# Wider products, a filter split by channels, filter sums on TensorE and whole x * v units per engine, in a fused long convolution and gated MLP

## The chip, the cores and the metric

One core of one Trainium2 chip. The metric is the device time of one execution in microseconds (us). Engines are named as the profile names them: PE is TensorE's matmuls, PEld its weight loads, DVE is VectorE, ACT ScalarE, POOL GpSimd, SP the engine that issues the DMAs. A ratio is the mean time of one kernel's fast runs over that of the other's fast runs of the same rounds, so it is not quite the ratio of the medians beside it. A difference of under 2% counts as "same".

## The reference, cut to what matters

```python
u = x * v                                    # 4 batches x 12480 positions x 128 channels, fp32
h = relu(pos_emb @ w1) @ w2 * exp(-0.01*pos) # the filter, one for all batches
y = irfft(rfft(u, 2*S) * rfft(h, 2*S))[:S]   # a long convolution for each channel
z = (x * y).reshape(49920, 128)
g = z @ w_in;  out = (g * cos(g)) @ w_out    # d_ff = 2048: "the MoE"
```

The kernel does the convolution as a two-level transform. In its **first step** (`f1`) it multiplies by a cosine and sine table. In the **second step** (`f2`) it multiplies by a table `w` that differs for each row `k`, and takes the complex product with the filter's spectrum `h`. The **third step** (`i1`) and the **last** (`i2`) go back. The filter's and batch 0's second steps run together (the **joint** second step) and leave `w` and `h` in DRAM. Batches 1 to 3 load them again and run interleaved with the MoE of the batches before (the **later** second steps).

## The kernel before: the parts that the change and the argument touch

```python
def u_load(pool, bufs, b, a):                # bufs is 3: three x buffers, two v buffers
    for name, src, n in (("xt", x, bufs), ("vt", v, bufs - 1)):
        ...                                  # one DMA each
def u_sums(u, tiles, a):                     # sum on GpSimd, difference on VectorE
    for place, op, e in ((a, ALU.add, nc.gpsimd), (ODD + a, ALU.subtract, nc.vector)):
        e.tensor_tensor(...)
first_u = u_units(0, 3, slots[0:R, :, :, :], # who multiplies which half of x * v
                  lambda j, half: nc.vector if half and j % 3 and j < 18 else nc.gpsimd)

def f2_mm(ps, w, k1, i, filt=False):         # 2 rows k per unit
    ...
    elif k < KF:                             # filter: one product of 256 columns
        nc.tensor.matmul(pi, w[:, i, :], both, start=True, stop=True)
    else:                                    # or two of 128
        for r, src in enumerate((ftile[0:KE, :, k, :], above[0:KE, :, k - KF, :])):
            nc.tensor.matmul(pi[:, r * D:(r + 1) * D], w[:, i, :], src, ...)

def f2_product(pool, ps, h, k1):             # each yield ends a step of the interleaving
    t = pool.tile([N2, 2, CB, 2, 2], F32, name="t", bufs=1)
    for r, op in ((0, ALU.subtract), (1, ALU.add)):
        nc.vector.tensor_tensor(y[:, r], uu[:, 0], hh[:, r], op=ALU.mult)
        yield
        nc.vector.tensor_tensor(t[:, r], uu[:, 1], hh[:, 1 - r], op=ALU.mult)
        nc.gpsimd.tensor_tensor(y[:, r], y[:, r], t[:, r], op=op)
        yield
# joint step: w has 2 buffers and is stored to DRAM, h has 3 and is stored too
```

In the later second steps the code between two yields is a piece of the interleaving: a unit has four, and they are spread over 2.9 steps of the MoE (`F2_STEPS` in the kernel), so most steps of the MoE have one piece beside them and some two. The MoE's chain crosses all engines: PE `ph`, ACT `a`, DVE `k`, POOL `f`, ACT `cs` (the sine), DVE `gt`, PE `acc`. At the end of each block of rows ACT copies `acc` out as `ot`.

## Time and profile before

| | us |
|---|---|
| time, median of 4 runs | 3785.55 (3782.77 to 3786.09) |
| span of the profiled run, granted clock | 3783.9, 0.994 |
| tables start on POOL, after x * v | 96.9 |
| batch 0's first step goes on (PE) | 121.3 |
| joint second step starts; third step starts | 170.5; 272.7 |
| later second steps of batches 1, 2, 3, first to last matmul | 288.2, 288.6, 287.1 |

The stage marks are the start times of a stage's first and last matmul in the trace. The lines of the profile before stand in the prediction below.

### The profile page before, as it was taken

What the parts mean: (1) busy time and instruction counts of PE and PEld (TensorE: products, weight loads), DVE (VectorE), ACT (ScalarE), POOL (GpSimd) and SP (SyncE); (2) the same over time, 40 slices, a digit from 0 to 9 for tenths busy, and PEclk for the clock granted to TensorE, in tenths of its full rate; (3) what the DMA queues carried; (4) which work ended last, traced back from release to release, by engine and by line L of the source; (5) the groups of instructions that cost most, each with busy time, mean ns of one, the idle gap of its engine ahead of it and who ended that gap; (6) DMA issues with size and microseconds to landing.
All of it is one profiled execution on the core that took longest, in us unless ns stands there. A gap on an engine that the chain in (4) does not pass through costs nothing.

```text
span 3783.9 us, 47244 instructions
## 1 busy us (share of the span) xinstructions
PE 3704.6 (98%) x13546; PEld 2108.5 (56%) x13546; DVE 2774.6 (73%) x5658; ACT 2525.1 (67%) x4683; POOL 2594.2 (69%) x2342
## 2 busy tenths in 40 slices
PE   8898999999999999999999999999999999999999
PEld 6777555655466555555565556555566544444444
DVE  8887887688866777788766786788765566666666
ACT  5756776766665557766655567666664677777777
POOL 7666886488854665688745664788644577777776
PEclk9999999999999999999999999999999999999999
DMA  6253542022202550122203540122105200000000
GB/s 166 70 178 100 151 148 60 16 72 78 75 18 66 177 162 27 32 78 77 60 18 109 173 127 18 52 78 76 41 12 167 87 20 21 17 20 20 17 22 14
DMA packets 209499, 276.14 MB, mean 73 GB/s; under 512 B 17111, under 2 KB 146535, under 8 KB 209111
## 3 DMA queue, kind: packets, MB, share of 16 engines
q1 hardware_dynamic: 209239, 273.12, 24.4%
q8 instruction: 109, 1.79, 0.2%
q14 instruction: 151, 1.24, 0.1%
HBM read 193.64 MB, written 79.42 MB: 72 GB/s over the span
## 4 chain that ended last, share of the span: by engine, by line
PE 84%; POOL 7%; DVE 4%; ACT 2%; issue 2%; DMA 1%; SPq 0%; POOLq 0%; DVEq 0%; ACTq 0%
PE ph L727 31%; PE acc L752 26%; PE cv L752 5%; PE cv L491 5%; PE cv L466 4%; POOL f L736 4%; PE cv L402 3%; PE cv L442 3%; PE ph L126 2%; PE ps L402 2%; PE ps L442 1%; DVE k L733 1%; POOL slots L461 1%; ACT cs L741 1%; POOL tm L295 1%
## 5 line engine op out<-in xcount | busy, mean ns | idle before, releaser
L736 POOL TENSOR_TENSOR f<-a,k 128x512 f32<-128x512 f32 (+1 forms) x1568 | 1988.6, 1268 | 1049.6 <-DVE k L733 1048.6
L727 PE MATMUL ph<-at,w_in_sb 128*128 128x512 f32 (+1 forms) x3136 | 1601.0, 592 | 5.3 <-DVE gt L743 4.7
L730 ACT ACTIVATE a<-ph,quarter 128x512 f32<-128x512 f32 (+1 forms) x1568 | 1073.3, 685 | 751.1 <-PE ph L727 742.1
L752 PE MATMUL acc<-gt,w_out_sb 128*128 128x512 f32 (+1 forms) x2688 | 1373.6, 592 | 10.4 <-ACT ot L758 9.9
L743 DVE TENSOR_TENSOR gt<-ph,cs 128x512 f32<-128x512 f32 (+1 forms) x1568 | 1077.8, 687 | 318.9 <-ACT cs L741 291.6
L733 DVE TENSOR_SCALAR k<-a 128x512 f32<-128x512 f32 (+1 forms) x1568 | 772.7, 493 | 619.0 <-ACT a L730 597.8
L741 ACT ACTIVATE cs<-f 128x512 f32<-128x512 f32 (+1 forms) x1568 | 980.5, 625 | 338.1 <-POOL f L736 335.5
L752 PEld LDWEIGHTS acc<-gt,w_out_sb 128*128 128x128 f32 x2688 | 505.6, 189 | 663.5 <-issue 619.3
L727 PEld LDWEIGHTS ph<-at,w_in_sb 128*128 128x128 f32 x3136 | 554.1, 190 | 338.3 <-issue 266.6
L461 POOL TENSOR_TENSOR slots<-slots,t 120x256 f32<-120x256 f32 x384 | 311.7, 818 | 60.6 <-DVE t L460 40.1
L491 PEld LDWEIGHTS cv<-slots,tm 96*104 96x104 f32 x1920 | 240.4, 170 | 109.8 <-issue 82.6
L491 PE MATMUL cv<-slots,tm 96*104 96x128 f32 x1920 | 254.7, 275 | 9.8 <-DVE tm L291 4.9
L752 PE MATMUL cv<-gt,w_out_sb 128*128 128x512 f32 (+1 forms) x448 | 224.5, 583 | 0.7 <-DVE gt L743 0.7
L466 PEld LDWEIGHTS cv<-cs,slots 120*96 120x96 f32 x1536 | 176.7, 167 | 67.6 <-issue 65.7
L466 PE MATMUL cv<-cs,slots 120*96 120x120 f32 x1536 | 183.1, 266 | 0.0
L442 PE MATMUL cv<-slots,w 124*120 124x256 f32 x576 | 173.0, 380 | 0.0
L442 PEld LDWEIGHTS cv<-slots,w 124*120 124x120 f32 x576 | 103.6, 184 | 123.8 <-issue 110.9
L402 PEld LDWEIGHTS cv<-c,slots 104*124 104x124 f32 x768 | 132.5, 192 | 71.2 <-issue 58.3
L402 PE MATMUL cv<-c,slots 104*124 104x192 f32 x768 | 151.2, 326 | 4.8 <-DVE gt L743 3.5
L752 PEld LDWEIGHTS cv<-gt,w_out_sb 128*128 128x128 f32 x448 | 84.9, 190 | 104.5 <-issue 99.5
L390 DVE TENSOR_TENSOR xt<-xt,vt 104x256 f32<-104x256 f32 x177 | 137.9, 787 | 0.0
L476 DVE TENSOR_TENSOR slots<-cv,other 96x240 f32<-96x240 f32 x384 | 133.7, 394 | 4.2 <-ACT other L474 4.2
(129 smaller groups left out, 2586.9 us busy)
## 6 DMA issues: line engine op xcount, KB each, us to landing
h<-hd SPq DMA_DIRECT2D x144, 240.0 KB
tm<-td SPq DMA_DIRECT2D x96, 312.0 KB
xt<-in_x_dram SPq DMA_DIRECT2D x120, 208.0 KB
vt<-in_v_dram SPq DMA_DIRECT2D x120, 208.0 KB
xs<-in_x_dram SPq DMA_DIRECT2D x120, 208.0 KB
zd<-zs SPq DMA_DIRECT2D x119, 208.0 KB
zb<-zd SPq DMA_DIRECT2D x96, 256.0 KB
w<-wd SPq DMA_DIRECT2D x144, 116.2 KB
```

What stands on the lines that cost most here:

```text
L402: nc.tensor.matmul(ps[0:KE, i * 2 * N1:(i + 1) * 2 * N1], u[:, b, 0:KE, i], c1[0:u.shape[0], :, :].rearrange("p r k -> p (r k)"), start=Tr ...
L442: nc.tensor.matmul(pi, w[:, i, :], parts[0:KE, :, k], start=True, stop=True)
L461: nc.gpsimd.tensor_tensor(y[:, r], y[:, r], t[:, r], op=op)
L466: nc.tensor.matmul(ps[0:N1, (i * 2 + r) * N2:(i * 2 + r + 1) * N2], parts[0:N2, r, :, b, i], cs[:, r, :], start=True, stop=True)
L491: nc.tensor.matmul(ps[0:R, i * D:(i + 1) * D], t[:, i, r, :], slots[0:N1, :, place, :], start=(r == 0), stop=(r == 1))
L727: nc.tensor.matmul(ph[:, 0:m], w_in_sb[:, c * P:(c + 1) * P], ats[n][:, 0:m], start=True, stop=True)
L730: nc.scalar.activation(a[:, 0:m], ph[:, 0:m], AF.Identity, bias=quarter[:, 0:1], scale=INV_TWO_PI)
L733: nc.vector.tensor_scalar(out=k[:, 0:m], in0=a[:, 0:m], scalar1=ROUND, scalar2=ROUND, op0=ALU.add, op1=ALU.subtract)
L736: nc.gpsimd.tensor_tensor(f[:, 0:m], a[:, 0:m], k[:, 0:m], op=ALU.subtract)
L741: nc.scalar.activation(cs[:, 0:m], f[:, 0:m], AF.Sin, scale=TWO_PI)
L743: nc.vector.tensor_tensor(gt[:, 0:m], ph[:, 0:m], cs[:, 0:m], op=ALU.mult)
L752: nc.tensor.matmul(accs[n][:, 0:m], w_out_sb[:, c, :], gt[:, 0:m], start=(c == 0), stop=(c == NFC - 1))
```

## The change

The intent: fewer and longer VectorE instructions in the second step (two products of 512 for four of 256, read from PSUM with a step of 0), and a second `t` buffer. Fewer evictions of the filter's first step, by splitting its results by channels (so each row of the second step needs one matmul of 192 columns and one of 64). The filter's sums and differences by TensorE, with signed copies of `w2`. And x * v units that stay on one engine from multiplication to sums, so the engines don't wait for each other.

```diff
-        t = pool.tile([N2, 2, CB, 2, 2], F32, name="t", bufs=1)
+        t = pool.tile([N2, 2, CB, 4], F32, name="t", bufs=2)
+        for r, (dst, hh) in enumerate(((y, h[:, :, :, :]), (t[:, :, :, :], h[:, ::-1, :, :]))):
+            ...                          # twice: the same 256 columns of PSUM read for both halves
+            nc.vector.tensor_tensor(dst, twice, hh, op=ALU.mult)
+            yield
         for r, op in ((0, ALU.subtract), (1, ALU.add)):
-            nc.vector.tensor_tensor(y[:, r], uu[:, 0], hh[:, r], op=ALU.mult)
-            yield
-            nc.vector.tensor_tensor(t[:, r], uu[:, 1], hh[:, 1 - r], op=ALU.mult)
             nc.gpsimd.tensor_tensor(y[:, r], y[:, r], t[:, r], op=op)
             yield
 ...  # f2_mm: the filter's matmuls by channels
+        nc.tensor.matmul(pi[:, :, 0:NF], w[:, i, :], fout[...], start=True, stop=True)   # 192
+        nc.tensor.matmul(pi[:, :, NF:], w[:, i, :], far[:, q], start=True, stop=True)    # 64
 ...  # filter_hidden: one ReLU in two pieces; filter_out: sums by two matmuls, one eviction
 ...  # units of x * v
+                def taker(j):
+                    dve = j >= 5 and (j % 2 == 1 if j < 19 else j % 3 == 2)
+                    return nc.vector if dve else nc.gpsimd
+                first_u = u_units(0, 3, slots[0:R, :, :, :], lambda j, half: taker(j),
+                                  lambda j: (taker(j), taker(j)))
 ...  # two of the three inverse tables are loaded after the joint second step
```

## The prediction

> **What bounds the kernel now.** I read the busy shares and the 40 slices first, then a table of engine busy times by stage, then the chain of waits of the first 340 us, then the waits and the instructions in order of time of the two stages that the change touches.
>
> ```profile
> PE 3704.6 (98%) x13546; PEld 2108.5 (56%) x13546; DVE 2774.6 (73%) x5658; ACT 2525.1 (67%) x4683; POOL 2594.2 (69%) x2342
> ...
> PE   8898999999999999999999999999999999999999
> ```
>
> PE is busy throughout, except in the first slices. The table by stage (columns: stretch, its length, busy time of PE, PEld, DVE, ACT, POOL with counts, granted clock, DMA share, GB/s) says the same with edges that I put where the work changes: loads, x*v and the filter's layers (to 63.6), filter's first step (to 96.9, and to 121.3 beside tables made by POOL), first step of batch 0 (to 169.7), second step of filter and batch 0 together (to 273.4), then the third step and the long mixed part.
>
> ```profile
> 19.20:63.60 44.40, 35.45 (x159) 23.68 (x158) 38.82 (x97) 18.73 (x45) 38.08 (x42) 0.98 0.56 164
> 63.60:96.90 33.30, 32.44 (x178) 31.20 (x179) 30.51 (x95) 24.95 (x111) 29.28 (x39) 0.93 0.51 145
> 96.90:121.30 24.40, 15.47 (x84) 13.02 (x82) 20.92 (x78) 14.02 (x60) 19.34 (x50) 0.90 0.05 15
> ...
> 169.70:264.80 95.10, 92.33 (x457) 71.09 (x457) 86.62 (x270) 57.53 (x142) 61.84 (x88) 0.98 0.60 174
> ...
> 640.00:3783.90 3143.90, 3127.35 (x10782) 1699.87 (x10780) 2246.97 (x4394) 2098.28 (x3628) 2119.87 (x1795) 1.00 0.21 62
> ```
>
> From 640 us on PE is 99.5% busy: there a cheaper DVE or POOL instruction buys nothing. From 339 to 640 the chain of waits runs over POOL's f and tm, which the change does not touch. So the change can act only on about 340 us, and 2% (75.7 us) would be a fifth of that.
>
> Up to 121 us the slow thread is x*v of batch 0 followed by the tables, both on POOL:
>
> ```profile
> 85.49 1.42 POOL L390 TENSOR_TENSOR xt<-xt,vt 104x256 f32<-104x256 f32 x2
> 86.98 0.79 POOL L396 TENSOR_TENSOR slots<-xt 104x256 f32<-104x256 f32 x1
> 88.00 1.60 POOL L390 TENSOR_TENSOR xt<-xt,vt 104x256 f32<-104x256 f32 x2 [0.23 <-DMA vt<-in_v_dram]
> 89.68 0.80 POOL L396 TENSOR_TENSOR slots<-xt 104x256 f32<-104x256 f32 x1
> 91.08 1.41 POOL L390 TENSOR_TENSOR xt<-xt,vt 104x256 f32<-104x256 f32 x2 [0.60 <-DMA vt<-in_v_dram]
> ```
>
> POOL goes from unit to unit in 2.4 to 3.1 us, now with a short wait for v. The last add ends at 96.5; the tables then take POOL 23 us (96.9 to 119.8), ACT waits for each of them ("tw_t <- POOL turned" 4.7 us, "cs" 3.2, "rows" 2.1 in the list of waits), and PE, with all banks full, waits 7.08 us and starts batch 0's first step at 121.3. DVE and PE are not what ends this stage.
>
> The second step from 170 to 264 has a period of 2.02 us per pair of rows:
>
> ```profile
> 230.75 1.42 POOL L461 TENSOR_TENSOR slots<-slots,t 120x256 f32<-120x256 f32 x2 [0.60 <-DVE t L460]
> 230.85 0.41 DVE L460 TENSOR_TENSOR t<-ps,h 120x256 f32<-120x256 f32 x1
> ...
> 231.32 0.59 DVE L291 SCALAR_TENSOR_TENSOR w<-even,tw_w,ps 124x120 f32<-124x120 f32 x2
> ...
> 231.71 0.28 PEld L442 LDWEIGHTS ps<-slots,w 124*120 124x120 f32 x2 [0.19 <-DVE w L291]
> ...
> 231.82 0.42 DVE L458 TENSOR_TENSOR slots<-ps,h 120x256 f32<-120x256 f32 x1
> ...
> 232.20 0.42 DVE L460 TENSOR_TENSOR t<-ps,h 120x256 f32<-120x256 f32 x1
> ```
>
> Two loops have that length. First: t has one buffer; a product into t (0.42), 0.13 to POOL, two sums (1.42), 0.05 back to the next t: 2.02. Second: w has two buffers; making both halves (0.59), the store's issue, its landing 3.2 to 3.3 us later in most units of this stage (2.9 at its start), 0.1 to DVE: 3.7 to 4.05 for two units, so 1.85 to 2.02. PE's own work is four pairs of matmuls 0.44 apart: 1.76.
>
> **What the Trainium skill says.** "VectorE: DVE Perf Modes", section on the SBUF-source errata: an fp32 tensor_tensor takes (N+151)/0.96 ns. That is 424 ns for 256 and 691 for 512; the trace has 414 for the products of 256 and 690 for 128x512 with a PSUM operand (L743): it agrees. "SBUF — State Buffer", section "SBUF: two separate sides": VectorE with two SBUF inputs and GpSimd exclude each other for a whole instruction. The trace agrees: POOL's add (L396) takes 0.73 alone and 0.97 beside DVE's, DVE's 0.43 and up to 0.95. "DMA: Bandwidth & Descriptors", section "Anatomy of one DMA": a fixed cost of about 2 us, mostly the write's receipt. First parts of h's stores land 2.4 us after issue here, the last 3.1 to 3.6. "TensorE: Matmul & The Clock Gate", section "Wait — 56ns, not 53.3ns?": start to start is N/2.4 GHz + 2.5 ns, never under 25 ns. Each fp32 matmul here is two instructions, and passes of 128 columns (L448) start 0.11 us apart, 256 columns 0.22: twice the columns' cycles.
>
> **The change part by part.**
>
> Products of 512. Per pair of rows four DVE products of 256 become two of 512. Back to back the trace starts products of 256 every 0.335 us, so four cost 1.34; one of 512 by the same overhead is 0.60 (estimate: 512/0.96 ns + 67 ns), two 1.20. DVE per unit of the joint stage: 0.50 for w + 1.20 = 1.70. t gets two buffers, so the first loop is gone. Left are PE, DVE at 1.70, POOL at 1.42 and the loop of w's store, which is not changed. PE: two pairs of 256 for u (0.88), and for the filter two of 192 (0.325 each by the trace's 192-column pairs) and two of 64 (0.11 each, estimate from the columns): 0.87; 1.75 together. I take 1.95 as the new period, near the store's loop, which earlier landings let breathe a little: 48 x 0.07 = 3.4 us. At the end of the stage the last DVE product and POOL sum end 7.0 us after the last w (266.33 to 273.35); with 0.5 + 2 x 1.20, the last h at 2.95, 1.2, 0.13 and 1.42 that becomes 5.7: 1.3 us. Together 4.7 us. In the three later second steps the DVE saving (144 x 0.14 = 20 us of busy issue time) lies under a full PE: nothing.
>
> Filter's results by channels. Five evictions become three: DVE from 1.37 us per unit to 1.14 (trace's batch pattern: 0.55 and two at 0.28 after it), ACT from 1.17 to 1.0; share to ACT from 0.53 to 0.6. DVE falls from 41 to 29 us, ACT stays near 39. DVE, ending at 117.3, was not last; POOL's tables were: no direct gain.
>
> Filter's sums on PE. DVE loses 60 adds x 0.41 = 24.6 us and gains 15 copies (6 us); ACT's 30 copies of 0.37 become 45, its 11 ReLUs of 0.57 become 22 on 64 partitions, and 4 small scalings come: +13 us, where it has 18.7 of 44 busy. PE streams the same 120 x 128 columns x 2 = 26 us. x*v paces this stage, since DVE's evictions stand between its units in order: hidden. The split ReLU may start it 1 us later.
>
> A unit by one engine. POOL had 48 multiplies and 30 adds, and gets 19 units of four: 76. DVE 42, then 44. The amount is the same; gone are waits such as POOL's on DVE's half (0.42, 8 times, 4.9 us up to 63). But v has two buffers: its next load is issued when the unit two before is multiplied. One engine doing both halves takes 1.5 us, plus 3.2 for the load, so two units need 4.75 against 4.7 to 4.9 now. Working down the 30 units by that rule, POOL ends at about 94 instead of 96.5: 2.5 us.
>
> Tables loaded after the second step: up to 3 us later, before ACT needs them a little into the third step: +0.5 us.
>
> Sum: 4.7 + 2.5 - 0.5 = 6.7 us off, 3779. These estimates take no credit for calmer queues, so I shade it to 3777.
>
> **The rivals.**
> - The store's loop stays at 2.02: nothing from the second step but its tail. For it: in the second half DVE's w starts 0.1 us after w's landing, and denser traffic (174 GB/s now) may land later. Time 3783.
> - PE becomes the bound at 1.75 to 1.8, if landings return to the 2.9 us seen at the start: 48 x 0.25 = 12 us, total 3770. With an x*v thread 8 us shorter: 3763.
> - DVE and POOL exclude each other more often, as whole units now run beside each other: x*v ends 5 us later, tables with it: 3784 to 3788.
> - PE writes the second step's results in pairs with gaps. If that halved the rate, 192 units x 0.88 = 169 us would come on top, 3950. Against it: no gapped output is in the trace, but fp32 passes already take two cycles a column, so I give this 2%.
>
> **Range and chances.** The first two rivals span 3763 to 3783, the third reaches 3788. I predict 3777, with 3764 to 3787 eight times in ten. Faster by over 2% needs 76 us out of 340 us: 0.01. Slower by over 2% only by gapped writes or a stage gone wrong: 0.02. Within 2%: 0.97.
>
> **What would show it.** Right: products of 512 at about 0.69 us; period of the joint stage 1.85 to 2.0, with DVE's w waiting for w's store and no wait of t on POOL; POOL's tables starting at 92 to 96 and batch 0's first step 1 to 2 us after their end; PE's pairs in later second steps still 0.44; the span from the third step on unchanged within 2 us. Wrong: tables starting before 88 or after 100, a joint period of 1.75 or still 2.02, a third step that waits for its tables by more than 3 us, or a longer PE time after 640 us.

## The result, and the profile after

The changed kernel took 3813.47 us (3810.88 to 3815.73, 4 runs) against 3785.55: a ratio of 1.0075, 95% interval 1.0058 to 1.0092. By the 2% rule that is the same, as predicted. But it is 28 us slower where 9 us off was predicted, and outside the range.

The page of the changed kernel (busy times, PE's 40 slices, and the engines' shares of the chain that ended last):

```profile
PE 3716.5 (98%) x13762; PEld 2140.6 (56%) x13762; DVE 2753.2 (72%) x5154; ACT 2523.3 (66%) x4662; POOL 2576.1 (68%) x2339
...
PE   7898999999999999999999999999999999999999
...
PE 74%; POOL 11%; DVE 5%; ACT 4%; DMA 3%; issue 2%; SPq 0%; POOLq 0%; DVEq 0%; ACTq 0%
```

The same line of the chain in the kernel before:

```profile
PE 84%; POOL 7%; DVE 4%; ACT 2%; issue 2%; DMA 1%; SPq 0%; POOLq 0%; DVEq 0%; ACTq 0%
```

The busy shares hardly differ, and DVE has less to do (2753 us for 2775). Only the chain shows something: a tenth of the span moved from PE to POOL, DMA, ACT and DVE. The table by stage of the changed kernel (stretch, length, busy times, clock, DMA share, GB/s), with edges at the same kinds of work as in the prediction:

```profile
19.20:71.00 51.80, 41.54 (x280) 34.42 (x279) 22.79 (x47) 30.78 (x74) 32.26 (x44) 0.90 0.50 138
71.00:109.00 38.00, 32.20 (x172) 31.15 (x172) 24.02 (x60) 26.41 (x78) 24.80 (x35) 0.90 0.48 134
...
650.00:3808.90 3158.90, 3131.30 (x10776) 1702.12 (x10774) 2256.80 (x4104) 2085.99 (x3625) 2113.11 (x1795) 1.00 0.21 61
```

The two stages up to the tables now take 89.8 us instead of 77.7, and in both DVE and POOL are less busy (DVE 46.8 us in all instead of 69.3, POOL 57.1 instead of 67.4). Much of DVE's difference is work that the change took away (the filter's sums and two of five evictions); POOL has nearly as many operations as before, and the lists of waits below show that both engines wait longer. In the long mixed part PE is idle for 27.6 us (3158.9 - 3131.3), where it was 16.6 in a stretch of nearly the same work before.

The marks, from each kernel's start (the two right columns are lengths):

| mark | before | after | moved |
|---|---|---|---|
| filter's first step starts | 63.6 | 71.0 | +7.4 |
| tables start on POOL | 96.9 | 109.1 | +12.2 |
| batch 0's first step goes on | 121.3 | 133.3 | +12.0 |
| joint second step starts | 170.5 | 181.4 | +10.9 |
| third step of batch 0 starts | 272.7 | 283.5 | +10.8 |
| last step of batch 0 starts | 338.7 | 349.6 | +10.9 |
| later second step, batch 1 | 288.2 long | 292.8 long | +4.6 |
| later second step, batch 2 | 288.6 long | 292.0 long | +3.4 |
| later second step, batch 3 | 287.1 long | 291.0 long | +3.9 |
| end of the span | 3783.9 | 3808.9 | +25.0 |

So there are three findings: 11 us were lost before the joint second step; the joint step gained nothing; and the three later second steps lost 11.9 us together. The other 2 us are the net of small shifts: 2.1 us come back before batch 1's second step, and about 3 are lost after batch 3's.

**At the start.** The list of waits from 19 to 125 us (total, times, longest) of the kernel before, and of the changed one:

```profile
POOL xt L390 <- DMA vt<-in_v_dram: 18.9, 9, 15.9
```

```profile
POOL xt L395 <- DMA vt<-in_v_dram: 41.7, 12, 16.2
DVE xt L395 <- DMA vt<-in_v_dram: 26.6, 9, 4.4
```

One wait of 16 us is the very first load. Beyond it POOL waited 3 us for v before (and DVE not at all), and the two engines together wait 52 us after. The chain of waits of the changed kernel (start, length, what) shows the loop:

```profile
78.20 2.97 DMA vt<-in_v_dram
...
81.30 1.58 POOL xt L395 x2
82.90 2.76 DMA vt<-in_v_dram
...
85.79 1.42 POOL xt L395 x2
```

A v load lands, POOL multiplies both halves, that frees the buffer, and the next v load starts. The sums (1.4 us) lie beside the load. From 60 to 110 us the v loads make up 56.5% of this chain and POOL's multiplications 23.5%; POOL's sums and DVE's work on the filter's results come in between at 75 us and from 92 us on.

**In a later second step.** POOL in order of time (start, length, operation, idle before), before and after:

```profile
897.79 0.76 POOL L461 TENSOR_TENSOR slots<-slots,t 120x256 f32<-120x256 f32 x1 [0.19 <-DVE t L460]
898.90 1.28 POOL L736 TENSOR_TENSOR f<-a,k 128x512 f32<-128x512 f32 x1 [0.36 <-DVE k L733]
900.13 0.94 POOL L461 TENSOR_TENSOR slots<-slots,t 120x256 f32<-120x256 f32 x1
901.03 1.27 POOL L736 TENSOR_TENSOR f<-a,k 128x512 f32<-128x512 f32 x1
```

```profile
904.32 1.27 POOL L749 TENSOR_TENSOR f<-a,k 128x512 f32<-128x512 f32 x1 [0.76 <-DVE k L746]
905.54 1.63 POOL L473 TENSOR_TENSOR slots<-slots,t 120x256 f32<-120x256 f32 x2
907.12 1.27 POOL L749 TENSOR_TENSOR f<-a,k 128x512 f32<-128x512 f32 x1
```

Before, the two sums stand between different MoE subtractions; after, they come together, 1.6 us at once. The waits of batch 1's second step, before and after:

```profile
ACT cs L741 <- POOL f L736: 47.1, 102, 1.0
PE acc L752 <- ACT ot L758: 1.0, 2, 0.7
```

```profile
ACT cs L754 <- POOL f L749: 69.7, 110, 1.4
PE acc L765 <- ACT ot L771: 3.8, 6, 1.1
```

ACT waits 23 us longer for POOL's `f`, and PE, which has one accumulator for the MoE, waits longer for ACT to copy it out. Two theories came from this: **A**, the adjacent sums on POOL; **B**, the adjacent products of 0.68 us on DVE, which hold up `k` and `gt`. For the start: **U**, units by one engine with few buffers, against **F**, the filter's new form, which itself runs longer (its hidden layer's last matmul starts at 35.4 us instead of 29.7).

### The profile page after: what moved, and what is told of

Read it like the earlier page. It is cut to its first block, busy times and chain, and to the rows that moved or that the text cites.

```text
span 3808.9 us, 47014 instructions
## 1 busy us (share of the span) xinstructions
PE 3716.5 (98%) x13762; PEld 2140.6 (56%) x13762; DVE 2753.2 (72%) x5154; ACT 2523.3 (66%) x4662; POOL 2576.1 (68%) x2339
## 4 chain that ended last, share of the span: by engine, by line
PE 74%; POOL 11%; DVE 5%; ACT 4%; DMA 3%; issue 2%; SPq 0%; POOLq 0%; DVEq 0%; ACTq 0%
PE ph L740 28%; PE acc L765 24%; POOL f L749 7%; PE cv L765 5%; PE cv L503 4%; PE cv L478 4%; PE cv L407 3%; POOL slots L473 2%; PE ph L129 2%; PE cv L454 2%; ACT cs L754 2%; DMA wd<-w 1%; DVE gt L756 1%; DVE k L746 1%; DMA vt<-in_v_dram 1%
## 5 line engine op out<-in xcount | busy, mean ns | idle before, releaser
L746 DVE TENSOR_SCALAR k<-a 128x512 f32<-128x512 f32 (+1 forms) x1568 | 805.2, 514 | 638.3 <-ACT a L743 608.7
L473 POOL TENSOR_TENSOR slots<-slots,t 120x256 f32<-120x256 f32 x384 | 312.0, 823 | 57.1 <-DVE t L470 40.9
```

Source lines behind the costliest of these rows:

```text
L746: nc.vector.tensor_scalar(out=k[:, 0:m], in0=a[:, 0:m], scalar1=ROUND, scalar2=ROUND, op0=ALU.add, op1=ALU.subtract)
```

## The experiments

How well do the marks repeat? Kernels with the same code up to the joint step begin it within 1.1 us of each other (E1, E7, E8: 170.9, 172.0, 171.8) or within 2.6 (E6, E9, E13: 164.8, 167.4, 167.4). The later second steps repeat better: the eight other kernels with products of 256 in the old order have a sum of the three between 863.4 and 864.0 us (before: 863.9), and E1, E2, E6, with the change's product, 875.6, 876.4 and 876.6 (the changed kernel: 875.8). So a difference of over 1 us in that sum means something, though each kernel has only one trace. All of it in one table (ratio: to the kernel before):

| kernel | median us | ratio, 95% | joint step starts | later second steps | their sum |
|---|---|---|---|---|---|
| before | 3785.55 | | 170.5 | 288.2 288.6 287.1 | 863.9 |
| changed | 3813.47 | 1.0075 (1.0058 to 1.0092) | 181.4 | 292.8 292.0 291.0 | 875.8 |
| E1 units shared | 3799.59 | 1.0039 (1.0026 to 1.0051) | 170.9 | 292.5 292.0 291.1 | 875.6 |
| E2 third v buffer | 3820.42 | 1.0093 (1.0077 to 1.0108) | 188.9 | 292.8 292.1 291.4 | 876.4 |
| E3 before + whole units | 3812.4 | 1.0068 (1.0055 to 1.008) | 196.0 | 288.4 288.5 286.9 | 863.8 |
| E4 sums spaced | 3809.83 | 1.0058 (1.0045 to 1.007) | 179.4 | 291.8 291.3 288.8 | 871.9 |
| E5 before, grouped | 3836.57 | 1.0133 (1.0119 to 1.0147) | 169.4 | 300.4 305.4 302.9 | 908.7 |
| E6 five x, five v | 3795.17 | 1.0028 (1.0018 to 1.0037) | 164.8 | 293.0 292.3 291.3 | 876.6 |
| E7 E1 + 256 later | 3785.69 | 1.0 (0.9992 to 1.0009) | 172.0 | 288.3 288.7 287.0 | 864.0 |
| E8 E1 + 512 wide | 3790.78 | 1.0015 (1.0008 to 1.0022) | 171.8 | 291.1 287.4 289.8 | 868.3 |
| E9 E6 + 256 later | 3781.98 | 0.9985 (0.9979 to 0.9992) | 167.4 | 288.2 288.5 287.1 | 863.8 |
| E10 E9, filter by rows | 3781.12 | 0.9988 (0.9981 to 0.9994) | 167.2 | 288.1 288.5 286.9 | 863.4 |
| E11 E10 + third w | 3782.6 | 0.9992 (0.9984 to 1.0) | 168.0 | 288.1 288.5 287.1 | 863.6 |
| E12 E9 + third w | 3783.51 | 0.9993 (0.9985 to 1.0001) | 165.5 | 288.1 288.5 287.0 | 863.5 |
| E13 E6 + 256 in E8's places | 3788.08 | 1.0001 (0.9992 to 1.0009) | 167.4 | 290.3 287.7 289.0 | 867.0 |
| E14 before + five, five | 3784.3 | 0.9993 (0.9984 to 1.0001) | 168.9 | 288.1 288.9 286.9 | 863.9 |
| E15 E9, units shared | 3782.88 | 0.9987 (0.998 to 0.9994) | 169.3 | 288.1 288.5 287.0 | 863.6 |

### E1: the changed kernel, x * v units shared as before

```diff
-                first_u = u_units(0, 3, slots[0:R, :, :, :], lambda j, half: taker(j),
-                                  lambda j: (taker(j), taker(j)))
+                first_u = u_units(0, 3, slots[0:R, :, :, :],
+                                  lambda j, half: nc.vector if half and j % 3 and j < 18
+                                  else nc.gpsimd)
```

> The changed kernel with one part undone: the x*v units of the first batch are shared between GpSimd and VectorE inside each unit again, as before (GpSimd the sum and one or both multiplies, VectorE the difference). Theory U (the 11 us lost up to the first batch come from giving a whole unit to one engine, whose next unit then waits for a v load that was issued only when a buffer came free): TensorE resumes the first batch's first step at 122 to 125 us after the start instead of 133, and the time falls to 3801 to 3806 us from 3813. Rival F (the filter's own part is longer, with its split ReLU and sums on TensorE, and sets the resumption): TensorE resumes at 130 or later and the time stays at 3810 or more. Both: the later second steps lose their 4 to 5 us each as in the changed kernel.

PE went on with batch 0's first step at 123.3 us, and the joint step began at 170.9, as before the change. U holds, F falls: the filter's hidden layer still started its last matmul at 35.0 us, but that delay is made up by the joint step. Units by one engine cost the whole loss at the start.

### E2: one more v buffer, loads one unit earlier

```diff
-        for name, src, n in (("xt", x, bufs), ("vt", v, bufs - 1)):
+        for name, src, n in (("xt", x, bufs), ("vt", v, bufs - (side != "left" or b > 0))):
...
-                             ahead=bufs - 2)
+                             ahead=bufs - 2 + (b == 0))
```

> The changed kernel with a third v buffer for the first batch's x*v units and the loads issued one unit earlier (the small weight table moved into unused slots to make room). Units still by one engine. Theory U in its form 'the wait for the v load is the cost': GpSimd's waits for v loads in the x*v thread fall from about 40 us to under 10, TensorE resumes at 120 to 126 us instead of 133, time 3800 to 3807. Rival (the engines' own work and order is the cost, the load wait only fills what GpSimd would wait anyway): resumption at 130 or later, time 3810 to 3814.

A miss for both theories: 7 us slower than the changed kernel, and POOL's wait for v grew from 41.7 to 46.4 us. The reason I found in the order of the loads: issued a unit earlier, x of unit j needs the x buffer of unit j - 3, whose sums must be done, and that unit is mostly the other engine's. SP issues loads in order, so v stands behind that x. SP's waits for POOL's sums, which free x buffers, rose from 25.7 us to 59.3, which fits. Two loops had been tied into one. The experiment deepened one of two buffers.

### E3: the kernel before, with units by one engine alone

The edit is the change's own `taker` and `u_sums(..., engines)` on the kernel before.

> The kernel before with only the unit of x * v by one engine. Theory U: TensorE resumes the first batch's first step 8 to 12 us later than before (129 to 133 instead of 121), time 3793 to 3798 against 3785. Rival F (the loss needs the filter's new form): within 3 us of before, 3783 to 3788. The later second steps stay as in the kernel before in both.

The sign is U's, the size two to three times what was expected: PE went on with batch 0's first step at 145.7 us, the joint step began 25.5 us later and the time rose by 25 us. POOL and DVE together waited 81.1 us for v. My reading, not tested: without the filter's sums on PE, DVE has its old evictions between its units, and a late multiplication on DVE delays the next load. So this part alone is worse than in the change; the filter's new form hid more than half of it. The later second steps stayed at 863.8: what they lose doesn't come from here.

### E4: the sums two steps apart, products of 512 kept

```diff
             nc.vector.tensor_tensor(dst, twice, hh, op=ALU.mult)
-            yield
+            if r == 0:
+                yield
         for r, op in ((0, ALU.subtract), (1, ALU.add)):
             nc.gpsimd.tensor_tensor(y[:, r], y[:, r], t[:, r], op=op)
             yield
+            if r == 0:
+                yield
```

> The changed kernel with the two sums on GpSimd in the second step set two steps apart (first product; second product and first sum; nothing; second sum) instead of in adjacent steps; the products of 512 stay. Theory A (two adjacent sums of 1.4 to 1.6 us each hold up the MoE's subtraction on GpSimd, ScalarE's sine behind it and the eviction of the accumulator): the second steps of batches 1 to 3 lose at most 1 us each against the kernel before, time 3800 to 3804, 10 to 13 us below the changed kernel. Rival B (VectorE's long products, one behind the other, are what holds up the MoE): no change, 3811 to 3815. In both the first batch's joint second step stays within 2 us of 99.

Theory A gave a third of what it promised: the sum of the later second steps fell by 3.9 us (875.8 to 871.9), where it needed 12. The sums stand here in the steps of the kernel before (second and fourth), so the remaining 8.1 us come with the products: two of 0.68 us in the first two steps instead of four of 0.41, one in each.

### E5: the kernel before, its products of 256 grouped as the change groups them

```diff
             nc.vector.tensor_tensor(y[:, r], uu[:, 0], hh[:, r], op=ALU.mult)
-            yield
             nc.vector.tensor_tensor(t[:, r], uu[:, 1], hh[:, 1 - r], op=ALU.mult)
-            nc.gpsimd.tensor_tensor(y[:, r], y[:, r], t[:, r], op=op)
             yield
+        for r, op in ((0, ALU.subtract), (1, ALU.add)):
+            nc.gpsimd.tensor_tensor(y[:, r], y[:, r], t[:, r], op=op)
+            yield
```

> The kernel before, its 256-column products kept, but grouped as the changed kernel groups them: two products, two products, first sum, second sum, each pair in its own step. Theory A/B (the order, adjacent long work on VectorE then GpSimd, holds up the MoE, not the new form of the product): the second steps of batches 1 to 3 lose 3 to 5 us each and the time is 3793 to 3802. Rival C (the loss comes from the product of 512 itself or from the new layout of the accumulator in PSUM): the later second steps stay within 1 us of before, time 3783 to 3788 (a shift of up to 3 us in the joint step apart).

The order alone, with the old form and the old layout, costs 12.2, 16.8 and 15.8 us: rival C falls, and the effect is three to four times what I expected. Batch 1's waits show a new one besides the known ones:

```profile
ACT cs L742 <- POOL f L737: 91.6, 122, 1.7
DVE t L459 <- POOL slots L462: 12.3, 11, 1.1
```

With one `t` buffer, a unit's first product into `t` now comes in its first step, right after the step with the last sum that reads the old `t` on POOL, and DVE stands. The changed kernel has a second `t` buffer and doesn't show this line. How the 45 us divide between that wait and the grouping is not settled.

### E6: five x and five v buffers

The v tiles and the small weight table go into columns of `slots` that are unused at that time, so five x and five v tiles fit; loads are issued three units ahead.

```diff
-        for name, src, n in (("xt", x, bufs), ("vt", v, bufs - 1)):
+        for name, src, n in (("xt", x, 5 if deep else bufs), ("vt", v, bufs - 1)):
+            if deep and name == "vt":
+                c = 4 * (j % 5)
+                t = slots[0:R, c:c + 4, KE:KE + CB, :].rearrange(...)   # two DMAs, one per half
...
-                             ahead=bufs - 2)
+                             ahead=3 if b == 0 else bufs - 2)
```

> The changed kernel, units still by one engine, with five x and five v buffers for the first batch (v in unused columns of the slots) and loads issued three units ahead; the run with one more v buffer failed because its x buffers then became the limit. Theory U' (a unit on one engine holds its buffers for four operations, 2.84 us on GpSimd, and the next load starts only when they come free): GpSimd's waits for v loads in the x*v thread fall from 42 us to under 25 (16 of it the first load), TensorE resumes at 110 to 123 us instead of 133, time 3795 to 3804. Rival (order of engines): 3810 or more.

It did what E2 couldn't. PE went on at 117.5 us instead of 133.3, the joint step began at 164.8, 5.7 us earlier than in the kernel before, and the time fell by 18 us. POOL's wait for v up to 135 us, nearly all of it the first load:

```profile
POOL xt L408 <- DMA slots<-in_v_dram: 20.9, 7, 15.4
```

The pace of the units (from the start of one unit's first multiplication to the next's) puts a number on it: before, 2.46 us for units 4 to 18 and 2.62 for 18 to 29; changed, 2.95 and 3.03; E3, 3.36 and 3.57; E6, 2.31 and 2.43.

### E7: E1, with products of 256 in the old order in the later second steps

```diff
+    def f2_product_256(pool, ps, h, k1):
+        for r, op in ((0, ALU.subtract), (1, ALU.add)):
+            nc.vector.tensor_tensor(y[:, r], u[:, 0], h[:, r], op=ALU.mult)
+            yield
+            nc.vector.tensor_tensor(t[:, r], u[:, 1], h[:, 1 - r], op=ALU.mult)
+            nc.gpsimd.tensor_tensor(y[:, r], y[:, r], t[:, r], op=op)
+            yield
```

> The changed kernel with x*v units shared as before (which gave 3799.6) and the second steps of batches 1 to 3 with products of 256 in the old order (product, product and sum, product, product and sum); the new layouts and the joint step of 512 stay. Theories A and B: the later second steps return to within 1 us of before each (288.2, 288.6, 287.1), time 3784 to 3789. Rival C' (the layout of the accumulator or the table loads cost it): they stay at 291 to 292.8, time 3798 to 3802.

The later second steps went back to 864.0 us and the time to that of the kernel before. The accumulator is still written to PSUM with gaps here, in the change's layout, so the layout costs nothing. Batch 1's waits are those of before again: ACT waits 46.3 us for POOL's `f` (47.1 before, 69.7 in the changed kernel), PE 1.0 us for the accumulator's copy (1.0 and 3.8).

### E8: E1, with products of 512 two steps apart

```diff
             nc.vector.tensor_tensor(dst, twice, hh, op=ALU.mult)
+            if r == 0:
+                yield
+                yield
         ...                      # and the sums two steps apart as in E4
```

> As the run with products of 256 later, but the later second steps keep the products of 512, set two steps apart, and the sums two steps apart: product, nothing, product and sum, nothing, sum. Theory B' (what counts is that no two long operations of one engine stand in adjacent steps): later second steps within 1 us of before, time 3784 to 3790. Rival B (a single product of 0.68 us on VectorE is already too long for the MoE's chain): they lose 2 to 4 us each, time 3792 to 3800.

Between the two: 4.4 us lost in the sum (2.9, -1.2, 2.7), time 3790.8. Spreading the long products gives back most of the loss; not all.

### E13: E6, with products of 256 and the sums in E8's places

```diff
+        nc.vector.tensor_tensor(y[:, 0], ...);  yield
+        nc.vector.tensor_tensor(y[:, 1], ...);  yield
+        nc.vector.tensor_tensor(t[:, 0], ...);  nc.gpsimd.tensor_tensor(y[:, 0], ...);  yield
+        nc.vector.tensor_tensor(t[:, 1], ...);  yield
+        nc.gpsimd.tensor_tensor(y[:, 1], ...);  yield
```

> As the run with both repairs (five buffers, products of 256 later), but the products of 256 of the later second steps in the order that the widened run with products of 512 gave its sums: product into y, product into y, product into t and first sum, product into t, second sum, one product a step at most, the sums two steps apart but half a unit later than before. Theory L (length: one product of 512 takes 0.68 us in one go on VectorE where one of 256 takes 0.41, and the MoE's chain there has no room for it): the later second steps stay within 1 us of 288.2, 288.6 and 287.1, time 3779 to 3784. Rival P (place: what costs is that the sums come late in the unit, near the next unit's products): they lose 1 to 4 us each as with the widened 512, time 3785 to 3793.

With short products in E8's places, the loss is 3.1 us (2.1, -0.9, 1.9), in E8's pattern batch by batch. In both runs the second sum stands in the same piece as the next unit's first product. So of E8's 4.4 us, 3.1 belong to the order with its late sums and 1.3, which is little more than the scatter, to the length of the products and their place. P holds: a product of 512 as such costs the MoE little. What costs is where the long work stands.

### E9: both repairs together

E6 with E7's product.

> The changed kernel with both repairs: five x and five v buffers for the units of x * v by one engine, and products of 256 in the old order in the second steps of batches 1 to 3. If the two causes are separate and add (18 us from the one, 14 from the other): 3813 - 32 = 3781, range 3777 to 3784, so 2 to 8 us below the kernel before. If they are not separate (the gain at the start is lost again on the way): 3784 to 3788.

The two causes add: 3781.98 us, ratio 0.9985 (0.9979 to 0.9992). It beats the kernel before by 0.15% and the changed one by about 31 us (medians of different rounds).

### E10, E11, E12: what bounds the joint second step

E10 is E9 with the filter's `f1_evict_filter` and `f2_mm` as before (by rows), E11 adds a third `w` buffer to E10, E12 adds it to E9:

```diff
-                ws[j] = pool.tile([KE, 2, N2], F32, name="w")
+                ws[j] = pool.tile([KE, 2, N2], F32, name="w", bufs=3)
...
-            cs = third_table(lpool)              # no room: loaded after the joint step
+            cs, (rows, tw_t) = third_table(wpool), last_tables(wpool)
```

> As the one with both repairs, but the filter's first-step results split as before (by rows of the result: one product of 256 columns for the first 48 rows, two of 128 for the others) instead of by channels (192 and 64 columns). Theory M (in the joint second step TensorE itself is the bound at 1.946 us a unit, because the weights after a matmul of 64 columns load in the open): TensorE is no longer full in the joint step and its period falls to 1.85 to 1.95, where the w store binds, so 2 to 6 us off its 98.6 us. Rival W (the w store's landing is the bound in both): the period stays at 1.98 to 2.03, the step within 2 us of 98. The filter's own part changes by under 2 us. Time within 6 us of the run with both repairs.

> As the one with rows, with a third w buffer in the joint second step (the third step's table is loaded after that step to make room). Theory M: with the store out of the way and no matmul of 64 columns the period falls to TensorE's own 1.76 to 1.85, the joint step to 86 to 91 us, the time to 3768 to 3776. Rival (VectorE's or GpSimd's own chain binds at 2.0): the step stays at 96 to 99.

> As the one with both repairs, by channels, with a third w buffer. Theory M: TensorE at 1.946 us a unit is the bound, so all of the joint step runs at 1.94 to 1.96 instead of 1.95 to 2.1: 93 to 96 us instead of 98.6, no less; time 3776 to 3780. Rival W: the store was the bound, and the period falls below 1.90, the step under 92.

Period by period, the trace shows what each kernel is held by (distance of the first matmuls of two units):

| kernel | first two units | then |
|---|---|---|
| before | 3.19, 2.04 | 1.74 for four units, then 2.02 |
| changed | 3.82, 2.73 | 1.95 for 19 units, then 2.01 to 2.03 |
| E10 rows | 3.54, 2.18 | 1.74 for six units, then 2.02 |
| E11 rows, third w | 3.54, 2.80 | 1.74 for nine units, then 2.01 |
| E12 channels, third w | 3.82, 2.45 | 1.95 for 42 units |

Each kernel starts at PE's own pace, 1.74 us by rows and 1.95 by channels, until something catches it at about 2.02. (Single longer periods, up to 2.8, are left out.) E12 looks like M's run: 1.95 almost throughout; but the step is 96.8 us long, just above the 93 to 96 expected, and the time missed its range. E10 and E11 missed M's ranges: without matmuls of 64 columns PE is no longer the bound, but the period stayed at 2.02 (as W had it for E10, with a step of 97.9 us), even with three `w` buffers. The waits of the joint step, for the kernel before, the changed one and E11:

```profile
ACT h L614 <- DMA hd<-h: 28.9, 37, 1.2
...
DVE w L291 <- DMA wd<-w: 4.4, 4, 3.0
...
DVE t L460 <- POOL slots L461: 0.2, 1, 0.2
```

```profile
DVE w L296 <- DMA wd<-w: 8.6, 32, 1.0
...
ACT h L627 <- DMA hd<-h: 3.7, 3, 1.4
```

```profile
ACT h L647 <- DMA hd<-h: 32.0, 36, 1.4
```

In the kernel before it is the store of `h`, three buffers deep: ACT waited for it 37 times in 48 units, DVE for `t` once. In the changed kernel PE's longer work and then the `w` store take its place. No run has a fourth `h` buffer, and a wait for a store need not mean that a buffer is missing.

The packed traces settle more than the waits do, since the updates of a store's semaphore tell when it landed. From the 9th to the 45th store of `w`, the landings take 74.0 to 74.2 us in the kernel before, the changed one, E9, E10 and E12, and 73.1 in E11, with a median of 2.01 to 2.02 us from one to the next: whatever PE's pace is and however many buffers there are. The third `w` buffer only lets the stores queue up. In the second half of E11 and E12 they land 4.7 us after they are issued, with two buffers 3.1; and E11 and E12, one by rows and one by channels, need the same 96.7 and 96.8 us. So what all these kernels run into is the rate at which the stores drain. PE can run ahead of it only as far as the buffers allow, and which store an engine waits for depends on which buffers run out first. The rate looks like that of a few DMA engines: a store of `w` updates its semaphore once about 0.5 us after the issue and four times at the landing, a store of `h` fifteen times at the landing; in E11 and E12 there are never fewer than four packets in flight (195 to 262 us, 205 to 258 us), and at the moments with exactly four, 95% and 93% of them are `w`'s packets of 960 bytes. I read this as four DMA engines that carry `w` without a pause. No run changes the stores themselves, so that last step is not tested. Rival W was right that the `w` store is the bound, but as a rate and not as a loop of two buffers.

Why PE's pace by channels is 1.95: PE in order of time in the changed kernel, then in E10.

```profile
204.01 0.49 PE L456 MATMUL ps<-ftile,w 124*120 124x192 f32 x2
204.34 0.32 PE L461 MATMUL ps<-slots,w 124*120 124x64 f32 x2
204.50 0.64 PE L454 MATMUL ps<-slots,w 124*120 124x256 f32 x2
204.98 0.49 PE L456 MATMUL ps<-ftile,w 124*120 124x192 f32 x2
```

```profile
177.32 0.59 PE L462 MATMUL ps<-slots,w 124*120 124x256 f32 x2
177.75 0.60 PE L466 MATMUL ps<-ftile,w 124*120 124x256 f32 x2
178.19 0.59 PE L462 MATMUL ps<-slots,w 124*120 124x256 f32 x2
```

Read the starts, since the ends are modelled. In E10 a pair of 256 columns starts every 0.43 or 0.44 us, four to a unit: 1.74. By channels 192 columns take 0.33, 64 take 0.16 and the 256 behind them 0.48, or 0.97 a row and 1.95 a unit. By their columns the 64 should take 0.11 and the 256 0.44. The Trainium skill, "TensorE: Matmul & The Clock Gate", section "LDWEIGHTS (loading the stationary operand)", gives a weight load in ns as the number of weight columns over 1.2, an estimate of 100 ns for 120. The trace agrees: behind a matmul of 64 columns three loads start 0.101 and 0.104 us apart, back to back. A pass of 64 columns (0.055 us) is shorter than the load of the next pass, so the load shows, twice a row.

E12's faster joint step (96.8 us from its first to its last matmul, against 99.2 in E9) didn't reach the time. The third step's table now came after the joint step, and PE waited for the tables (the profile names the last one that landed):

```profile
PE ps L503 <- DMA rows<-rowsd: 7.6, 1, 7.6
```

In E9 PE waits 2.9 us at that place, for POOL's last sums. The room for the buffer was paid for with that wait.

### E14 and E15: are the buffers the gain, or units by one engine?

E14 is the kernel before with E6's buffers; E15 is E9 with units shared as in E1.

> The kernel before with nothing of the change but five x and five v buffers for the first batch's x * v, its units shared between the two engines as they were. Theory N (the gain of the repaired start is that of the buffers, and the kernel before waits for v loads too, 18.9 us of GpSimd's and VectorE's time): TensorE starts the joint second step at 164 to 168 us instead of 170.5 and the time falls by 3 to 6 us, 3779 to 3783. Rival O (the gain needs units by one engine): the start stays within 1.5 us of 170.5, time 3784 to 3788.

> As the run with both repairs, but units shared between the engines as before: with enough buffers, is a unit by one engine better, equal or worse? Theory O: the joint step starts at 169 us or later, against 167.4 and 164.8 with units by one engine, time 3784 to 3787. Theory N: it starts at 163 to 168, time within 2 us of 3782.

Buffers alone moved the joint step's start by 1.6 us on the kernel before (168.9) and left it at 169.3 in E15; with units by one engine it was 164.8 to 167.4 in three runs, and 165.5 to 168.0 in E10 to E12. That speaks for O: given buffers, units by one engine bring the start some 1 to 5 us forward, which is not far from the scatter of 1 to 3 us. But E9, E15 and E14 lie within 2.3 us of each other in the median, with intervals that overlap, so the times don't settle it.

## Why the prediction was wrong, point by point

**x * v by one engine ("POOL ends at about 94 instead of 96.5: 2.5 us").** This step failed. POOL's tables began at 109.1, the joint step 10.9 us late. The prediction had seen the loop (v has two buffers, multiplication plus load for two units) and counted it at 4.75 us for two units, 2.375 for one. E6, with the loop gone, has 2.31 to 2.43, so as a count of the engines' work the figure was right. As the loop's, it was a best case: it took the multiplication to follow the landing at once. The units went at 2.95 to 3.03; in the chain of waits a landed v also waits for its own engine to finish the sums of its last unit or the evictions in front of it, and the next load waits with it. The prediction's own sign of being wrong, tables after 100 us, came. E1 (take the part away) and E6 (take the loop away) both give the loss back; E2 shows that half the buffers don't.

**"In the three later second steps the DVE saving lies under a full PE: nothing."** Also failed: 11.9 us lost. That a saving is worth nothing there was right. The prediction didn't ask what moving the work does, and it had said of this part only that PE is full. Two long products in adjacent pieces cost 8.1 us (E4), adjacent sums a further 3.9 (changed against E4), and neither the length of a product nor the layout costs much (E13, E7). That the delay reaches PE through ACT's copy of the accumulator is read from the waits of batch 1, not tested by itself.

**The joint step ("48 x 0.07 = 3.4 us" and the tail, 4.7 together).** Nothing came: 102.1 us from its first matmul to the third step's, before and after. This step failed too, in the loop of `w`'s store: the prediction counted making, issue and landing over two buffers, and let earlier landings shorten that to 1.95. The stores land every 2.01 to 2.02 us in every kernel, with one `t` or two and with two `w` buffers or three, so the first rival ("the store's loop stays at 2.02") is what happened. PE's work was mis-sized as well: put at 1.75, it is 1.95, since the 64-column matmuls were counted by columns alone. So the 1.95 chosen as the new period was met for 19 units by PE's own pace, while the four that ran at 1.74 before ran at 1.95 and the first two took 1.3 us longer (6.55 for 5.23). The tail did shrink, from 5.9 to 5.0 us from the start of the last unit to the third step.

**The filter's parts ("hidden", "may start it 1 us later").** Right in effect, wrong in size: the hidden layer's last matmul started 5.7 us later, and with units shared the joint step still began 0.4 to 1.5 us later than before (E1, E7, E8).

**Tables loaded later (+0.5).** Right, and smaller still: the third step took 66.1 us to the next stage, 66.0 before.

**The rivals.** Gapped writes to PSUM cost nothing, as the prediction leant: E10 writes with gaps, and its units start 1.74 us apart as long as PE sets the pace, as in the kernel before. (A matmul record in the later steps has a mean of 381 ns against 380, but its end is modelled.) DVE and POOL excluding each other: E6 has the same pairing and ends earlier, so it isn't the main cost; its own share stays open. None of the rivals named the order of work inside the MoE's steps or the queue in front of a landed v.

## What to carry to other kernels

When a buffer's owner changes, write down what frees it and count that loop with the owner's queue in it, not with the bare operation: giving a whole unit to one engine lengthened the hold on each buffer and cost 11 us until both inputs had more. The Trainium skill, "Perfetto Trace Analysis", section "Optimization Strategy", says that the same gap repeating can mean too few buffers; here POOL's repeated gap of 1.4 us before each unit agreed, and deepening only one of two buffers made it worse. A wait for a store's landing asks how fast the stores drain before it asks for a buffer: a third `w` buffer left the landings at 2.02 us a unit. Beside a pipeline that crosses all engines, spread the work evenly over its steps: fewer, longer instructions saved DVE time and cost 12 us by their place.

## What the Trainium skill lacked or had wrong

- "TensorE: Matmul & The Clock Gate", the section on weight loads, is right for this case (0.101 and 0.104 us between loads of 120 columns, 0.100 by its formula). What it lacks is a figure for matmuls of unequal width in a row: here, where an fp32 matmul is two loads and two passes, one of 64 columns among longer ones cost 0.16 us and made the next of 256 take 0.48 instead of 0.44.
- "PSUM — Partial Sum Buffer", section "Specifications (TRN2)", says that any non-contiguous pattern slows matmuls significantly, without a figure. Here results written to PSUM in runs of two elements, with gaps between them, cost nothing: pairs of 256 columns start every 0.43 to 0.44 us in E10 and units every 1.74 us, as in the kernel before.
- I found no figure for a VectorE product that reads the same PSUM columns twice by a step of 0: 0.680 us for 512, as long as one without it (0.690 for 128x512).
- "DMA: Bandwidth & Descriptors" has no figure for loads issued close together from one queue. In the changed kernel, after the first burst, a v load landed in 2.7 to 3.0 us when no other load had been issued in the 1.5 us before it (once in 4.3), and took up to 5.1 behind another pair issued within 1.5 us.
